# Attention and experts on one core: one written order for all engines per pair of heads

## The chip, the cores and the metric

The kernel runs on one core of a Trainium2 chip. The core has five engines that run side by side, each working through its own list of instructions in order: TensorE (PE in the profile, its weight loads PEld), VectorE (DVE), ScalarE (ACT), GpSimd (POOL) and SyncE (SP), which only issues DMAs. They wait for each other through semaphores. The metric is the time of one execution in microseconds (us), lower is better. TensorE's clock is granted at one of two levels, 1.2 or 2.4 GHz; the profile shows it as a share of full speed.

## The reference

Two stages follow each other. Attention has 8 batches of 8 heads, 576 tokens and head dimension 64; then a mixture of 8 experts picks one expert per token.

```python
    scores = scale * np.matmul(q, k.transpose(0, 1, 3, 2))
    log_f = np.log(np.clip(f, 0.0001, 1.0))
    cum = np.cumsum(log_f, axis=-1)
    decay = cum[:, :, :, None] - cum[:, :, None, :]
    scores = np.where(causal, -1000000000.0, scores + decay)
    scores = scores - np.max(scores, axis=-1, keepdims=True)
    attn = np.exp(scores)
    attn = attn / (np.sum(attn, axis=-1, keepdims=True) + 1e-09)
    return np.matmul(attn, v).astype(np.float32)
...
    logits = x @ w_gate
    expert_idx = np.argmax(logits, axis=1)
...
        h = np.maximum(xe @ w1[e], 0.0)
        ye = h @ w2[e]
        out[mask] = gate_w[mask, None] * ye
```

## The kernel before

Attention goes over 32 pairs of heads (`n` = 0 to 31, four pairs per batch), then the expert stage runs from about 450 us to the end. The change touches attention only, and the first steps of the expert stage that are mixed into its last pass.

The work of one pair has these pieces. The names in brackets are those of the new code, and this text uses them for both kernels.

- **Scores.** `s_tiles` (line 358) multiplies q with k for query tiles 3 (R1, 512 columns), 2 (R2, 384) and 1 with 0 (R3, 256 and 128), for both heads. `s_joint` (line 391) does the fifth, half-filled query tile of both heads together (J).
- **Row minima.** `reds` on DVE (line 342) reads each score bank, adds the decay bias, writes the result to SBUF tiles `sc` and leaves the row extreme in `nmx`. The names are r03 to r10 (head, tile), rj0 and rj1 for the joint tile.
- **Exponentials.** `exps` on ACT (line 377, joint tile 383): e03 to e10 and ej.
- **Turns.** The exponentials are transposed on PE in three groups of 16 half-turns (line 408): G1 (tile 3), G2 (tiles 2 and 1), G3 (the diagonal blocks and the joint tile). Each group fills two PSUM banks, which ACT or DVE copies to SBUF tile `aT` (line 420). One full turn of the joint tile (TL, line 403) is copied by DVE (tl, line 465).
- **Product with v.** `av` (line 475) writes two banks (AVa, AVb); ACT copies them to `xT` (line 483).

PSUM is handed out in a fixed rotation of seven banks (`next_bank`), so each piece that asks for banks waits until the bank taken seven requests earlier has been read.

The loop over `n` runs seven steps `s0` to `s6`. Per step it emits R1 with its minima (s0), G2 of the pair before (s1), R2 (s2), G3 of the pair before (s3), R3 (s4), TL and the product of the pair before, then J of this pair (s5), and G1 of this pair (s6). So on PE a pair reads: R1, G2, R2, G3, R3, TL, AV, J, G1. `order.pin()` after each step ties the instructions of each engine to the order in which steps were written; inside a step a scheduler chooses.

Behind the pieces of a pair come the tasks of the batch that was finished before (`fin_tasks`): the gate product (`fin_gate`, line 551), five tiles of normalised rows (`fin_x`, turns on PE and scaling on DVE at line 510), the gate's logits, softmax, expert choice, rank, slot, and the one-hot products `hi` (line 923 on DVE, then line 930 on POOL), `lo` (line 937) and `table` (line 944 on PE, added up on DVE at line 948). They are spread over four passes of the loop: of `n % 4`, 1 carries the gate, 2 two row tiles, logits, softmax and expert, 3 gate value, two row tiles, rank and slot, 0 the one-hots, the table and the last row tile. POOL also masks the bias of the next pair (lines 309 to 318) and splits q and k into two rounded parts (lines 293, 298).

## Time and profile before

| what | value |
|---|---|
| time, median of three runs | 890.74 us (889.8 to 891.26) |
| profiled execution, its own time | 893.72 us |
| its span, first to last instruction | 892.0 us |
| mean granted TensorE clock | 0.901 |
| PE busy | 838.8 us, 94% |
| DVE, ACT, POOL busy | 593.8, 478.4, 496.7 us |
| attention, first to last exponential of a joint tile | 17.7 to 428.3 us |

A row of the window view gives, for a stretch, its length and each engine's busy time; a busy engine may still be a slow one, since matmuls last longer at the lower clock. PEclk is the granted share of full clock in that stretch.

### The profile page before, as it was taken

The numbers are of one execution on the slowest core, as the hardware profiler recorded it, in microseconds if no ns is written. First come the engines' busy times: TensorE is split into PE (matmuls) and PEld (weight loads), VectorE is DVE, ScalarE is ACT, GpSimd is POOL, SyncE is SP. The second block draws the span as 40 slices with busy tenths as digits, with TensorE's granted clock in tenths as the row PEclk, the third lists the DMA queues.
The fourth block names the chain that finished last, engine by engine and source line by source line (L and its number), as shares of the span: only waits on it lengthen the run. The fifth ranks groups of instructions, "written<-read, shape, count | busy, mean of one in ns | idle before, by whom it ended". The sixth has DMA issues, their size and how long they took to land.

```text
span 892.0 us, 18923 instructions
## 1 busy us (share of the span) xinstructions
PE 838.8 (94%) x6640; PEld 683.5 (77%) x6640; DVE 593.8 (67%) x1707; ACT 478.4 (54%) x1216; POOL 496.7 (56%) x616
## 2 busy tenths in 40 slices
PE   5998999989989899898899999999999999999997
PEld 4676676666766666666788998988989899898985
DVE  6667676676776766767443887584966848588450
ACT  6775464655646546466353655554646546465430
POOL 6985472854628456366325676465755657566411
PEclk9998687877878778786799999999999999999999
DMA  7655353563644534445114453634335343443301
GB/s 189 168 150 150 109 160 102 133 163 96 161 116 134 159 100 146 146 137 174 58 64 147 124 164 98 198 96 141 84 111 178 95 159 86 128 128 107 115 12 41
DMA packets 78817, 112.15 MB, mean 126 GB/s; under 512 B 9343, under 2 KB 40063, under 8 KB 78720
## 3 DMA queue, kind: packets, MB, share of 16 engines
q1 hardware_dynamic: 71680, 90.97, 35.2%
q0 software_dynamic: 6400, 19.93, 6.9%
q8 instruction: 54, 0.88, 0.4%
q14 instruction: 43, 0.35, 0.1%
q10 hardware_dynamic: 640, 0.01, 0.0%
HBM read 91.85 MB, written 20.07 MB: 125 GB/s over the span
## 4 chain that ended last, share of the span: by engine, by line
PE 72%; DVE 13%; POOL 6%; issue 5%; DMA 2%; ACT 1%; ACTq 0%; DVEq 0%; SPq 0%; POOLq 0%
PE ps L1151 24%; PE ps L1349 16%; PE ps L475 13%; PE ps L358 5%; DVE sc L342 4%; PE ps L1121 4%; DVE aT L420 3%; PE ps L408 3%; PE ps L391 2%; PE ps L403 2%; DVE sc_J L342 2%; PE pr L1349 1%; POOL bias L309 1%; PE ps L1305 1%; POOL hl L298 1%
## 5 line engine op out<-in xcount | busy, mean ns | idle before, releaser
L377 ACT ACTIVATE sc<-sc,nmx 128x512 f32<-128x512 f32 (+3 forms) x256 | 143.4, 562 | 69.1 <-DVE nmx L342 67.2
L358 PE MATMUL ps<-hl 64*128 64x512 f32 (+3 forms) x768 | 124.4, 403 | 21.9 <-DVE nmx L342 14.0
L475 PE MATMUL ps<-aT,va_t 128*64 128x256 f32 (+3 forms) x896 | 128.2, 453 | 2.5 <-ACT sc L377 2.1
L1151 PE MATMUL ps<-w_0w,hhw 128*128 128x512 f32 x280 | 113.0, 404 | 0.0
L475 PEld LDWEIGHTS ps<-aT,va_t 128*64 128x64 f32 x896 | 74.8, 181 | 48.7 <-issue 27.9
L1349 PE MATMUL ps<-X_0w,w1s 128*128 128x320 f32 x504 | 111.7, 309 | 0.0
L1151 PE MATMUL ps<-w_0w,hl 128*128 128x512 f32 x280 | 110.9, 396 | 0.0
L1151 PE MATMUL ps<-w_1w,hhw 128*128 128x512 f32 x280 | 110.5, 395 | 0.0
L358 PEld LDWEIGHTS ps<-hl 64*128 64x128 f32 x768 | 80.9, 233 | 36.4 <-DVE nmx L342 14.2
L1159 POOL DMA_INDIRECT out<-y,si_fast x37 | 37.7, 1018 | 97.2 <-ACT y L1158 82.8
L420 DVE COPY aT<-ps 128x512 f32<-128x512 f32 (+1 forms) x160 | 87.7, 574 | 1.8 <-PE ps L408 1.6
L298 POOL TENSOR_TENSOR hl<-raw,hl 128x512 fp32r<-128x512 f32 (+1 forms) x62 | 83.3, 1344 | 5.1
L342 DVE CUSTOM_DVE_ANT_0 sc_J<-ps,bias 128x288 f32<-128x288 f32 x32 | 14.6, 458 | 105.4 <-PE ps L391 105.4
L1349 PEld LDWEIGHTS ps<-X_0w,w1s 128*128 128x128 f32 x504 | 84.3, 188 | 0.0
L1349 PE MATMUL ps<-X_1w,w1s 128*128 128x320 f32 x252 | 78.0, 310 | 0.0
L293 POOL CAST hl<-raw 128x512 fp32r<-128x512 f32 (+1 forms) x60 | 38.2, 637 | 62.1 <-DMA raw<-in_qkT 46.7
L1158 ACT ACTIVATE y<-ps,g_fast 128x512 f32<-128x512 f32 x37 | 25.5, 689 | 84.9 <-PE ps L1151 63.6
L483 ACT COPY xT<-ps 128x320 f32<-128x320 f32 x64 | 25.5, 399 | 80.6 <-PE ps L475 80.6
L930 POOL TENSOR_TENSOR Rr<-eqh,vals 128x240 bf16<-128x240 bf16 x35 | 19.4, 587 | 82.0 <-DVE eqh L923 82.0
L1151 PEld LDWEIGHTS ps<-w_0w,hl 128*128 128x128 f32 x280 | 52.5, 188 | 12.6
L1151 PEld LDWEIGHTS ps<-w_1w,hhw 128*128 128x128 f32 x280 | 52.9, 189 | 11.0
L1151 PEld LDWEIGHTS ps<-w_0w,hhw 128*128 128x128 f32 x280 | 52.6, 188 | 10.9
(240 smaller groups left out, 2033.3 us busy)
## 6 DMA issues: line engine op xcount, KB each, us to landing
bias<-ud SPq DMA_DIRECT2D x31, 576.0 KB, 5.6
w1r<-in_w SPq DMA_DIRECT2D x112, 128.0 KB, 3.4
w<-in_w SPq DMA_DIRECT2D x28, 512.0 KB, 5.0
raw<-in_qkT SPq DMA_DIRECT2D x64, 160.0 KB, 3.0
raw<-in_qkT SPq DMA_DIRECT2D x64, 144.0 KB, 3.0
va_t<-in_va SPq DMA_DIRECT2D x32, 256.0 KB, 5.7
x_dram<-row SPq DMA_DIRECT2D x32, 256.0 KB, 2.4
wraw<-in_w SPq DMA_DIRECT2D x7, 512.0 KB, 3.8
```

Of the source, the lines that this page charges most:

```text
L293: return eng(hls[n][:, 0, o : o + w], raws[n][:, r : r + w])
L298: return eng.tensor_tensor(hl[:, 1], raws[n][:, r : r + w], hl[:, 0].bitcast(F32), ALU.subtract)
L342: V.tensor_tensor_reduce(dst, src, in1, -0.125, init, ALU.add, ALU.min, nms[n][:, col : col + 1])
L358: note(nc.tensor.matmul(pb[j][:, o : o + w], hl[js, q, P * t : P * t + P], hl[js, k, 512 : 512 + w], start=(i == 0), stop=(i == 2),))
L377: A.activation(x, x, AF.Exp, bias=nms[n][:, 5 * j + t : 5 * j + t + 1], scale=-1.0, accum_out=ssums[b][:, t, 2 * p + j : 2 * p + j + 1])
L408: note(nc.tensor.transpose(out.bitcast(F32R), words, c.identr[rows, rows]))
L420: copy_on = {"a": lambda o, i: A.copy(o, i), "v": lambda o, i: V.tensor_copy(o, i)}
L475: note(nc.tensor.matmul(pv[j * HD : (j + 1) * HD, q0 - qa : qb - qa], l, r, start=(blk == 0), stop=(blk == nb - 1),))
L1121: c.note(nc.tensor.matmul(ph[:, 0:n], w[:, wi, fs], x[xi][:, kt, :], start=(k == 0), stop=(k == 3 * KT - 1),))
L1151: c.note(nc.tensor.matmul(py, rows(hi_, ft), w[wi], start=(ft + k == 0), stop=(ft == FT - 1 and k == 2),))
L1159: nc.gpsimd.indirect_dma_start(out=self.out, out_offset=bass.IndirectOffsetOnAxis(ap=si[:, s : s + 1], axis=0), in_=y, in_offset=None, bou ...
L1349: self.nc.tensor.matmul(bank[:, 0:HN], w[:, wi, mat, kt], x[xi][:, kt, :], start=start and k == 0, stop=k == 5, skip_group_check=True,)
```

## The change

The seven steps become one tuple `PERIOD` of about 55 entries, each a name, a lag in pairs (0 for this pair, 1 for the pair before) and a function. Every entry is emitted and pinned by itself, so the order inside a pair is now written out for all engines. Entries without a function (`at(...)`) are places where loads, masks, roundings and the tasks of the finished batch hang; a task carries the name of its place instead of a step number.

What the new order has that differs: G1 moves from the end of its own pair to the pass of the next pair, so that all three groups of turns are a pair late; on PE a pair reads R1, G1, R2, G2, G3, R3, J, TL, AVa, AVb. J now stands ahead of the product with v. Three exponentials (e01, e00, e10) are a pair late too. Of the bank copies, those of G1, G2 and all but one of G3 go to ACT and stand in one run ahead of this pair's exponentials; the two copies of the product with v go from ACT to DVE. The row tiles (`fx`) stand behind the product, softmax, expert and slot beside it (place V), logits, rank and table between R3 and J (place X), and the one-hots just ahead of the table in the same pass (place U). Row writes to DRAM wait six places instead of three steps, and five products of the first expert that were spread over the last pass stand at two places.

```diff
-            for half in range(2):
-                s_red(n, region(c.values, n, 0, -1)[:, half * JW : half * JW + JW],
-                      pb[half][:, 0:JW], added(n, half, -1), 10 + half,
-                      1.0e38 if half == 0 else nms[n][:, 10:11])
+                held[n, "j", half] = pb[half][:, 0:JW]
...
+        def av_last(n):
+
+            pvs[n] = [next_bank() for _ in range(2)][::-1]
+            lasts[n] = pvs[n][1][0:64, 256:384]
+            turn(lasts[n], region(c.words, n, 0, -1)[:, 512:S])
...
+        def av_out(n, part, eng):
             b, p = divmod(n, NPAIR)
...
+            qa, qb = ((0, 320), (320, S))[part]
+            copy_on[eng](xTs[b][:, p, qa:qb], pvs[n][part][:, 0 : qb - qa])
...
-                later.append([3, write])
+                later.append([6, write])
...
-                (0, 4, lambda: fin_gate(b)), (1, 4, lg[0]), (1, 4, lg[1]), (1, 5, softmax),
-                (1, 6, expert), (2, 0, gate), (2, 4, rank), (2, 5, slot), (2, 6, hi),
-                (3, 0, lo), (3, 4, table), (1, 1, fx[0]), (1, 3, fx[1]), (2, 1, fx[2]),
-                (2, 3, fx[3]), (3, 4, fx[4]),
+                (0, "X", lambda: fin_gate(b)), (0, "F", fx[0]), (0, "F", fx[1]),
+                (1, "X", lg[0]), (1, "X", lg[1]), (1, "V", softmax), (1, "V", expert),
+                (2, "U", gate), (2, "X", rank), (2, "V", slot), (3, "U", hi), (3, "U", lo),
+                (3, "X", table), (3 - 2 * late, "F", fx[2]), (3 - late, "F", fx[3]),
+                (3 - late, "C", fx[4]),
...
+        PERIOD = (
+            at(0), ("R1", 0, score(3)), ("e01", 1, power(0, 1)), ("e00", 1, power(0, 0)),
+            ("e10", 1, power(1, 0)), ("G1", 1, grouped(1, g_first)), at(1),
+            ("r03", 0, most(0, 3)), ("r13", 0, most(1, 3)), ("R2", 0, score(2)),
...
+        for n in range(NP + 1):
+            for name, lag, f in PERIOD:
+                if f is None:
...
+                    prepare(n, name)
+                    behind(n, name)
+                elif 0 <= n - lag < NP:
+                    step(lambda: f(n - lag))
                 order.pin()
...
-        return [lambda: moe.up(0, 0, i - 2)]
+        ups = {4: (0, 1, 2), 6: (3, 4)}.get(i, ()) if n == last + 1 else ()
+        return [lambda ft=ft: moe.up(0, 0, ft) for ft in ups]
```

The order that results is shown at three places. The first is PE in a pass with `n % 4` = 0, from the product with v on; `sc` are exponentials, `raw` unrounded q and k, `xT` the normalised rows' source, `hl` the rounded q and k. Before:

```order
L403 MATMUL ps<-identr,xT1w 64x128 x4
L403 MATMUL ps<-identr,sc_Jw 64x128
L475 MATMUL ps<-aT_97,va_t 64x320 x2
L475 MATMUL ps<-aT_97,va_t 64x192 x2
L475 MATMUL ps<-aT_97,va_t 64x64 x2
L475 MATMUL ps<-aT_97,va_t 64x256 x6
L475 MATMUL ps<-aT_97,va_t 64x192 x2
L475 MATMUL ps<-aT_97,vb_182 64x64 x2
L391 MATMUL ps<-raw 64x288 x4
L408 MATMUL ps<-identr,sc_03w 128x64 x8
L408 MATMUL ps<-identr,sc_13w 128x64 x8
L358 MATMUL ps<-hl 128x512 x6
```

The same place on PE in the changed kernel:

```order
L391 MATMUL ps<-raw 64x288 x4
L405 MATMUL ps<-identr,sc_Jw 64x128
L481 MATMUL ps<-aT_97,va_t 64x320 x2
L481 MATMUL ps<-aT_97,va_t 64x192 x2
L481 MATMUL ps<-aT_97,va_t 64x64 x2
L481 MATMUL ps<-aT_97,va_t 64x256 x6
L481 MATMUL ps<-aT_97,va_t 64x192 x2
L481 MATMUL ps<-aT_97,vb_182 64x64 x2
L405 MATMUL ps<-identr,xT1w 64x128 x4
L410 MATMUL ps<-identr,xT1w 128x64 x16
L358 MATMUL ps<-hl 128x512 x6
```

J moved from behind the product to ahead of it, the turns of G1 between J and R1 are gone from here (they stand behind R1 now), and three row tiles (`xT1w`) follow the product.

The second place is ACT in one plain pair, from its first exponential of tile 3 on. Before:

```order
L377 ACTIVATE sc_03_71,ssum<-sc_03_71,nmx 128x512
L420 COPY aT_91<-ps 128x2x2x2x64
L377 ACTIVATE sc_13_77,ssum<-sc_13_77,nmx 128x512
L420 COPY aT_91<-ps 128x4x64 x2
L377 ACTIVATE sc_02_73,ssum<-sc_02_73,nmx 128x384
L377 ACTIVATE sc_12_79,ssum<-sc_12_79,nmx 128x384
L377 ACTIVATE sc_01_75,ssum<-sc_01_75,nmx 128x256
L483 COPY xT_85<-ps 128x320
L377 ACTIVATE sc_11_81,ssum<-sc_11_81,nmx 128x256
L483 COPY xT_85<-ps 128x256
L377 ACTIVATE sc_02_73,ssum<-sc_02_73,nmx 128x128
L377 ACTIVATE sc_12_79,ssum<-sc_12_79,nmx 128x128
```

ACT in one plain pair of the changed kernel:

```order
L377 ACTIVATE sc_03_57,ssum<-sc_03_57,nmx 128x512
L377 ACTIVATE sc_11_67,ssum<-sc_11_67,nmx 128x256
L377 ACTIVATE sc_02_59,ssum<-sc_02_59,nmx 128x384
L377 ACTIVATE sc_13_63,ssum<-sc_13_63,nmx 128x512
L377 ACTIVATE sc_12_65,ssum<-sc_12_65,nmx 128x384
L383 ACTIVATE sc_J,jsum<-sc_J,nmx 128x576
L377 ACTIVATE sc_01_61,ssum<-sc_01_61,nmx 128x256
L377 ACTIVATE sc_02_59,ssum<-sc_02_59,nmx 128x128
L377 ACTIVATE sc_12_65,ssum<-sc_12_65,nmx 128x128
L422 COPY aT_91<-ps 128x2x4x64 x2
L422 COPY aT_91<-ps 128x2x2x2x64 x2
L422 COPY aT_91<-ps 128x4x64 x3
```

Five copies were strung between nine exponentials (three of `aT`, two of `xT`); now nine exponentials and seven copies of `aT` form two runs.

The third place is DVE in a pass with `n % 4` = 0, around the one-hots. Each minimum is followed by a small `nmx` row. Before:

```order
L420 COPY aT_97<-ps 128x2x4x64 x2
L923 TENSOR_TENSOR eqh<-pr,iotah 128x200
L650 MEMSET ssum 64x8
L342 ISA sc_03_57,nmx<-ps,bias 128x512
L342 ISA nmx 128x1
L342 ISA sc_13_63,nmx<-ps,bias 128x512
L342 ISA nmx 128x1
L937 TENSOR_TENSOR Ar<-pr,iota_601 128x640
L420 COPY aT_97<-ps 128x2x2x2x64
L420 COPY aT_97<-ps 128x4x64
L342 ISA sc_02_59,nmx<-ps,bias 128x384
L342 ISA nmx 128x1
```

DVE at the one-hots of the changed kernel:

```order
L342 ISA sc_12_65,nmx<-ps,bias 128x384
L342 ISA nmx 128x1
L913 TENSOR_TENSOR eqh<-pr,iotah 128x200
L927 TENSOR_TENSOR Ar<-pr,iota_606 128x640
L422 COPY aT_97<-ps 128x4x64
L938 TENSOR_TENSOR tab<-tab,pr 128x240
L342 ISA sc_02_59,nmx<-ps,bias 128x128
L342 ISA nmx 128x1
L342 ISA sc_01_61,nmx<-ps,bias 128x256
```

The one-hot `eqh` came ahead of the minima of tile 3 and the table's addition `tab` some twenty rows later; now `eqh` follows the minima of tile 2, and `tab` stands three rows behind it, ahead of the minima of tiles 0 and 1.

## Rows read from the trace of the kernel before

**Rows 1.** The page's slices: the span in 40 equal slices, busy share of PE and granted clock in tenths.

```profile
PE   5998999989989899898899999999999999999997
...
PEclk9998687877878778786799999999999999999999
```

**Rows 2.** The window view, one stretch per pair, from the joint tile's exponential of one pair to that of the next: length, then busy time (and count) of PE, PEld, DVE, ACT, POOL; granted clock, DMA share and GB/s. The first is an early pair without batch tasks, the others the four pairs of one batch (`n` = 17 to 20).

```profile
28.45:38.52 10.07, 9.05 (x117) 7.14 (x117) 7.11 (x27) 7.04 (x23) 9.54 (x18) 1.00 0.54 153
...
223.40:233.40 10.00, 9.78 (x131) 7.01 (x131) 7.01 (x27) 7.65 (x26) 6.44 (x10) 1.00 0.67 153
233.40:248.04 14.64, 13.84 (x146) 10.22 (x144) 10.49 (x41) 7.74 (x24) 8.52 (x13) 0.77 0.49 145
248.04:263.88 15.84, 13.73 (x131) 9.67 (x129) 11.15 (x49) 7.60 (x25) 3.91 (x4) 0.68 0.44 126
263.88:278.01 14.13, 12.86 (x124) 9.35 (x124) 9.80 (x38) 7.38 (x23) 11.15 (x19) 0.76 0.44 118
```

**Rows 3.** The view of line 383, the joint tile's exponential, one per pair: duration and first and last start.

```profile
L383 ACT ACTIVATE sc_J<-sc_J,nmx x32: 761/777/782, 17.7 to 428.3; 128x576 f32<-128x576 f32 x32
```

**Rows 4.** The window view again, the same batch cut at the turn TL (product with v and J follow it) and at the first turn of G1 (turns and scores follow it): columns as in rows 2.

```profile
222.50:228.46 5.96, 5.74 (x90) 4.44 (x88) 5.81 (x20) 4.32 (x14) 3.54 (x7) 1.00 0.54 142
228.46:232.48 4.02, 4.02 (x48) 2.55 (x41) 1.18 (x8) 3.31 (x13) 2.88 (x4) 1.00 0.86 170
232.48:240.73 8.25, 7.45 (x95) 6.38 (x94) 7.66 (x25) 5.38 (x16) 6.11 (x9) 0.80 0.55 142
240.73:246.39 5.66, 5.66 (x43) 3.27 (x42) 2.17 (x14) 2.23 (x9) 3.27 (x6) 0.69 0.41 155
246.39:256.92 10.53, 8.42 (x96) 6.78 (x95) 9.67 (x39) 5.36 (x16) 3.91 (x4) 0.72 0.63 170
256.92:263.01 6.09, 6.09 (x47) 3.50 (x45) 2.19 (x14) 2.38 (x9) 0.00 (x0) 0.64 0.11 43
263.01:271.20 8.19, 6.92 (x81) 5.85 (x80) 7.82 (x29) 4.90 (x14) 4.73 (x9) 0.81 0.62 161
271.20:277.09 5.89, 5.89 (x45) 3.46 (x43) 1.93 (x10) 2.47 (x11) 5.56 (x10) 0.68 0.21 59
```

**Rows 5.** The timeline of PE in the pair at 223 us: start, length, operation, count, idle time before it. A piece's length is read from one start to the next, since matmuls overlap.

```profile
223.16 0.97 PE L358 MATMUL ps<-hl 64*128 64x512 f32 x6
223.96 0.20 PE L408 MATMUL ps<-identr,sc_01w 64*128 64x64 f32 x2
...
224.55 0.80 PE L358 MATMUL ps<-hl 64*128 64x384 f32 x6
225.19 0.45 PE L408 MATMUL ps<-identr,sc_02w 64*128 64x64 f32 x4
...
226.52 0.91 PE L358 MATMUL ps<-hl 64*128 64x256 f32 x11 [0.22 <-DVE aT L420]
227.35 1.18 PE L551 MATMUL ps<-xT,wg 128*32 128x512 f32 x16
228.46 0.25 PE L403 MATMUL ps<-identr,sc_Jw 128*64 128x128 f32 x1
...
231.41 1.14 PE L391 MATMUL ps<-raw 128*64 128x288 f32 x8
```

**Rows 6.** Groups of ACT's copies in the pair from 48.42 to 58.52 us, shapes kept apart: count, busy us, mean ns, idle before.

```profile
L420 ACT COPY aT<-ps 128x256 f32<-128x256 f32 x2 | 0.6, 370 | 0.0
L420 ACT COPY aT<-ps 128x512 f32<-128x512 f32 x1 | 0.6, 566 | 0.0
L483 ACT COPY xT<-ps 128x320 f32<-128x320 f32 x1 | 0.4, 417 | 0.0
L483 ACT COPY xT<-ps 128x256 f32<-128x256 f32 x1 | 0.4, 372 | 1.2 <-PE ps L475 1.2
```

**Rows 7.** Groups of DVE's work in the same pair.

```profile
L420 DVE COPY aT<-ps 128x512 f32<-128x512 f32 x4 | 2.7, 688 | 0.0
L342 DVE CUSTOM_DVE_ANT_0 sc<-ps,bias 128x512 f32<-128x512 f32 x2 | 1.3, 688 | 0.0
L342 DVE CUSTOM_DVE_ANT_1 sc<-ps,bias 128x384 f32<-128x384 f32 x2 | 1.1, 548 | 0.0
...
L420 DVE COPY aT<-ps 128x256 f32<-128x256 f32 x2 | 0.8, 417 | 0.0
```

**Rows 8.** The one-hots and the table in the timelines of DVE, POOL and PE (start, length).

```profile
265.90 0.35 DVE L923 TENSOR_TENSOR eqh<-pr,iotah 128x200 bf16<-128x200 f32 x1
...
266.34 2.77 POOL L930 TENSOR_TENSOR Rr<-eqh,vals 128x240 bf16<-128x240 bf16 x5 [11.71 <-DVE eqh L923]
...
270.01 1.18 PE L944 MATMUL pr<-Rr,Ar 128*128 128x240 bf16 x5
```

**Rows 9.** The window view of three stretches of turns and scores: columns as in rows 2.

```profile
223.80:227.30 3.50, 3.28 (x54) 2.81 (x50) 3.50 (x11) 2.48 (x8) 1.30 (x4) 1.00 0.59 161
...
234.00:237.40 3.40, 2.90 (x51) 2.39 (x47) 3.29 (x9) 2.21 (x7) 1.56 (x4) 1.00 0.62 179
237.40:240.70 3.30, 3.00 (x28) 2.62 (x27) 2.96 (x11) 2.24 (x8) 3.14 (x4) 0.50 0.69 160
```

**Rows 10.** First and last instruction of softmax and expert choice in DVE's timeline (two copies of 1.28 us together lie between them).

```profile
247.19 0.20 DVE L848 TENSOR_REDUCE mx<-pr 128x5 f32<-128x40 f32 x1
...
249.96 0.21 DVE L870 CAST ohb<-pr 128x48 bf16<-128x48 f32 x1
```

More of the change, by code (lines that the diff above doesn't have):

```diff
@@ L395, in s_joint, with red_joint @@
                     ))
[L396 to L399 removed]
+                held[n, "j", half] = pb[half][:, 0:JW]
+        def red_joint(n, half):
+            s_red(n, region(c.values, n, 0, -1)[:, half * JW : half * JW + JW],
+                  held.pop((n, "j", half)), added(n, half, -1), 10 + half,
+                  1.0e38 if half == 0 else nms[n][:, 10:11])
         def turn(out, words):
@@ L481, in av_out, with out_last, av @@
-        def av_out():
-            A.copy(*pvs.pop(0))
+        pvs, lasts = {}, {}
+        def av_last(n):
+            pvs[n] = [next_bank() for _ in range(2)][::-1]
+            lasts[n] = pvs[n][1][0:64, 256:384]
+            turn(lasts[n], region(c.words, n, 0, -1)[:, 512:S])
+        def out_last(n):
+            V.tensor_copy(aTs[n][0:64, :, 1024:1088],
+                          lasts.pop(n).rearrange("p (j q) -> p j q", j=2))
+        def av(n, part):
+            va_t, vb_t = vts[n]
+            aT, pv = aTs[n], pvs[n][part]
+            qa, qb, nb = ((0, 320, 3), (320, S, 5))[part]
+            for blk in range(nb):
+                q0 = max(qa, P * blk)
+                for j in range(2):
+                    if blk < 4:
+                        l, r = va_t[:, blk, j, :], aT[:, j, AS * blk + q0 : AS * blk + qb]
+                    else:
+                        l, r = vb_t[:, j, :], aT[0:KB, j, 1024:1088]
+                    note(nc.tensor.matmul(
+                        pv[j * HD : (j + 1) * HD, q0 - qa : qb - qa], l, r,
+                        start=(blk == 0), stop=(blk == nb - 1),
+                    ))
@@ L638, in attention_all, with grouped, turned, score @@
         c.note = note
-        todo = None
-        for n in range(NP + 1):
+        todo, pts = None, {}
+        def grouped(k, f):
+            def turned(n):
+                pts[k, n] = f(n)
+            return turned
+        def score(*ts):
+            return lambda n: s_tiles(n, *ts)
+        def most(j, t):
+            return lambda n: reds(n, (j, t))
+        def power(j, t):
+            return lambda n: exps(n, (j, t))
+        def out(k, f, r, eng):
+            return lambda n: f(n, pts[k, n], r, eng)
@@ new lines, in prepare @@
+        def prepare(n, i):
+            if n + 2 < NP and i == 0:
+                load_raw(n + 2)
+            if n + 2 < NP and i == 2:
+                load_bias(n + 2)
+            if n == 0 and i == 0:
+                late_consts()
+                for part in (Q, K):
+                    rounded(1, A.copy, part)
+                for part in (Q, K):
+                    rest(1, G, part)
+            if n + 1 < NP and i == 1:
+                for f in selects(n + 1):
+                    f()
+            if n + 2 < NP and i in (3, 4):
+                part = (Q, K)[i - 3]
+                rounded(n + 2, G.tensor_copy, part)
+                rest(n + 2, G, part)
+            if i == 3 and 0 < n < NP:
+                load_v(n)
+            if i == 5 and n == 2:
+                load_gate()
+            if i in (2, 4) and 2 <= n < 5:
+                next(c.more, None)
@@ L641, in attention_all @@
             b, p = divmod(n, NPAIR)
-            new, old = n < NP, n > 0
-            m = n - 1
-            if new and p == 0:
+            if n < NP and (p, i) == (0, 0):
                 xTs[b], xTws[b] = (
@@ new lines, in behind @@
+        def behind(n, i):
+            nonlocal todo
+            b, p = divmod(n, NPAIR)
+            if n > 0 and (p, i) == (0, 0):
+                todo = fin_tasks(b - 1)
+            for f in tasks.pop((n, i), []):
+                step(f)
+            if n >= NPAIR:
+                if b == B:
+                    part = {1: 0, 3: 1, 5: 2}.get(i)
+                else:
+                    part = {(0, 1): 0, (1, 0): 1, (1, 4): 2}.get((p, i))
+                if part is not None:
+                    fin_sums(b - 1, part)
+            if (n, i) == (NP, 0):
+                scores.close()
+            if i in range(7):
```

153 lines of the change are left out of this document (23 added, 130 removed).

## The prediction

> **What bounds the kernel now.** I read the page's slices first: PE is busy in nine tenths of almost every slice, but its granted clock stands at 7 or 8 tenths from the fifth to the nineteenth slice, which is attention, and at full speed behind it [rows 1]. So the place to look is attention, and busy PE time there is partly slow PE time. The joint tile's exponential comes once per pair and runs from 17.7 to 428.3 us [rows 3]: 31 steps of 13.2 us on average. Cut by pairs, the window view shows what that mean hides. A pair with the clock at 1.00 takes 10.0 to 10.1 us, with batch tasks (223.40) or without (28.45); the other three of the same batch have a clock of 0.77, 0.68 and 0.76 and take 14.64, 15.84 and 14.13 [rows 2]. One batch is 54.6 us.
>
> Cut where the product with v begins and ends, each pair falls into a dense half (product and J: PE never idle) and a sparse half (turns and scores) [rows 4]. The dense half takes 4.02 us at full clock and 5.66, 6.09 and 5.89 in the other three pairs; the work is the same, so the clock costs 1.64 + 2.07 + 1.87 = 5.6 us per batch there. The sparse half takes 5.96, 8.25, 10.53 and 8.19 us, and in it DVE is busy for 5.81, 7.66, 9.67 and 7.82: 92 to 97%. In the dense half DVE is busy for only 1.2 to 2.2 us. So DVE bounds the sparse half, by minima, bank copies and batch tasks that all stand there, and then it sits idle while PE multiplies. PE's idle time in the sparse half is the other side of this.
>
> **What the clock does.** In the stretch 234.0 to 237.4 PE is busy for 2.90 of 3.40 us, with 51 matmuls that are mostly turns, and clock 1.00; in the next stretch it has 0.50 [rows 9]. At 223.8 PE is busy for 3.28 of 3.50 us with more score work, and the clock stays up in all of that pair. So what comes ahead of a fall is turns with waits between them, not idleness alone. The Trainium skill, "TensorE: Matmul & The Clock Gate", Part 4: PE-mode transpose, says that transposes do not count as PE activity in the way matmuls do; this trace agrees, with the 2.90 of 3.40 us just named. By the rule the new order, which sets G2 and G3 side by side, could lose the clock in every pair, which is worked out as the third rival (931 us); if PE's busy share alone decided, the clock would hold and the first rival's 806 us would follow.
>
> **The change part by part, for one batch.**
>
> PE's own work stays. From the starts in the pair at 223 us: R1 0.80, G2 0.59, R2 0.64, G3 0.73, R3 0.83, TL with the product 2.95, J 1.1 [rows 5], and G1, as many turns as G3, about 0.7. That is 8.3 us per pair at full clock. The batch tasks add the gate, 1.1 [rows 5]; four row tiles of 8 turns, half of G3 each, 1.5; the fifth, logits and rank, about 1.0 by their share of turns (estimate); the table, 0.6 (1.18 at half clock [rows 8]). So four pairs hold 33.2 + 4.2 = 37.4 us of PE.
>
> DVE loses three copies of 512 columns and one of 256, 3 x 0.688 + 0.417 = 2.48 us [rows 7], and gains two copies of the product, 320 and 256 columns. DVE has no copy of 320 in the trace; it lies between 0.417 and 0.688, I take 0.47. So 7.11 - 2.48 + 0.89 = 5.5 us in a plain pair. The batch tasks are what rows 2 show above 7.01: 3.48 + 4.14 + 2.79 = 10.4 us. Sum 4 x 5.5 + 10.4 = 32.5. What matters more is where: the minima of R3 and of J, both product copies, softmax, expert, slot and the row tiles now stand behind R3, in DVE's idle half.
>
> ACT gains three copies of 512 and one of 256 and loses two, 3 x 0.566 + 0.370 - 0.417 - 0.372 = 1.28 us [rows 6]: 7.04 + 1.28 = 8.3 us in a plain pair, 33.3 plus about 1 for gate and expert in a batch. POOL keeps its 6.44 + 8.52 + 3.91 + 11.15 = 30.0. So by work alone PE ends last, at 37.4, where 54.6 stand now.
>
> Then the waits that the fixed order adds; I followed one batch through the queues by hand, at full clock.
> - Pair with `n % 4` = 0: the one-hot on DVE now follows r12, so it ends about 3.8 us behind the start of R1 (R1 0.80, some 0.2 until DVE starts, two minima of 0.69 and two of 0.55, the one-hot 0.35 [rows 7, 8]). POOL needs 2.77 us more, until about 6.6. PE reaches the table at 0.80 + 0.70 + 0.64 + 0.59 + 0.73 + 0.83 = 4.3 and waits 2.3. Before, 3.8 us lay between the one-hot's end and the table [rows 8] and hid this. Behind the waiting table stand J and the product on PE, and behind `tab` on DVE the minima of R3, for which ACT's e11 waits too. Row tiles at the end hold a bank for another 0.4.
> - Softmax and expert, 250.17 - 247.19 - 1.28 = 1.7 us of DVE [rows 10], now stand ahead of rj1, so ej, then e01, e00, e10 and the copies of G1 are late by as much on ACT: G2, G3 and R3 of the next pair (`n % 4` = 3) wait about 1.2. Slot and gate value do the same to the pair after it, about 0.5, ahead of the table's wait.
> - A copy just ahead of AVa: 0.2.
>
> Waits 4.6 us, a batch of 42.0 at full clock. If the order hides all of them, 37.4; if each of the three pairs with routing waits as the table does (2.3, and 0.8 for what queues behind it), 37.4 + 9.3 = 46.7.
>
> Last the clock. The pair with the table has 2.3 us of waiting in turns and scores, so I expect it to lose the clock, and the one ahead of it (1.2 us of waits between G2 and G3) as well: two dense halves at 1.9 us more each [rows 4], 3.8, less a little that its ACT waits hide. The plain and the gate pair I expect at full clock: G1, R2, G2, G3 then follow each other without a wait between two score pieces. Bounds: 0 if it never falls, 5.6 if three dense halves stay as slow as today. I take 3.7: 42.0 + 3.7 = 45.7 us per batch.
>
> Pairs 6 to 31 are 6.5 batches: 6.5 x (54.6 - 45.7) = 58 us. The five early pairs run at full clock already; POOL is busy there for 9.54 of 10.07 us [rows 2], so I give them 3 us together. G1 of the last pair moves into the last pass (+0.7), which its five expert products, less scattered, may win back: 0. Row writes that wait longer, the other loads and GpSimd's masks keep their place ahead of need: 0, and at worst one wait of POOL for a bias, about 0.5.
>
> Sum against the profiled execution's 893.7: 893.7 - 58 - 3 = 832.7. That execution lies 3.0 above the median of the runs; at the median the forecast is 830 us. Between 43 and 48 us per batch it is 812 to 845.
>
> **Rivals.**
> 1. The clock holds throughout: 42.0 per batch, 893.7 - 6.5 x 12.6 - 3 - 3.0 = 806. For it: the pair at 223 us does hold its clock, with turns and a wait of 0.22 in it [rows 5], and DVE, which caused today's waits, is relieved. Against it: 2.3 us of waiting at the table.
> 2. The waits move rather than go: in-order queues pass DVE's routing chain on to ACT, which now does all copies ahead of its exponentials, and three pairs keep a slow dense half: 46.7 + 5.6 = 52.3, 893.7 - 6.5 x 2.3 - 6 = 873. For it: ACT at 8.3 us and PE at 8.3 in a plain pair leave no slack to either. Against: over a batch ACT has 8 us to spare below 42.0.
> 3. Slower: the clock falls in every pair, by turns standing side by side. Dense half 5.9 (mean of the slow three), sparse half with 2.3 us of score work doubled and 2.0 of turns kept, 6.6: 12.5 per pair, 50 per batch, plus tasks at half clock 4.2 x 1.5 and waits of 3, 59; early pairs 12.5 in place of 10.0. 893.7 + 6.5 x 4.4 + 5 x 2.4 - 3.0 = 931. Even at the lower clock part of this is hidden by waits. Time is lost from the point where a batch exceeds 54.6, three quarters of the way from 42.0 to 59. For it: [rows 9] and the page's rule on transposes. Against: R1 and R2 stand on both sides of G1, and the dense run of R3, J and product is one piece longer than today.
> 4. It does nothing, since another resource sets the end: POOL (30.0 of 54.6) and the DMA share of 0.44 to 0.67 [rows 2] do not look like it. 889 to 893.
>
> **How the numbers follow.** Forecast 50%, the first rival 18%, the second 15%, slower 13%, nothing 3%, better than all of these 1%. A difference below 0.2% (1.8 us, about the spread of the three runs) cannot be told from none. Faster holds forecast, first and second rival: 0.84; same 0.03; slower 0.13. The range reaches from below the first rival (40.0 per batch, 793) to just below the second (873): 792 to 872, which leaves out the slower side, nothing, and the tail below.
>
> **What would show it.** In the profile after, a batch of four pairs between 43 and 48 us; DVE's busy share of the sparse half well below 90%, and above half in the dense one; a wait of PE on POOL of about 2 us per batch at the table's line; waits of ACT for DVE in the pairs with softmax and gate value; two dense halves near 4.0 and two near 6 per batch. The forecast is wrong if the pairs without routing also show a clock below 1.00, if a batch stays above 50 us, or if PE waits for ACT's copies in every pair.

## The result, and the profile after

The changed kernel takes 809.41 us (median of 4 runs, 808.45 to 810.31), the kernel before 891.0 us on the same chip: a ratio of 0.9086, 95% interval 0.9071 to 0.9102. The forecast was 830 us, range 792 to 872. The profiled execution has a span of 807.3 us (892.0 before) and a mean granted clock of 0.979 (0.901 before).

The page's slices, PE busy and granted clock in tenths:

```profile
PE   5999999999999999969999999999999999999996
...
PEclk9999999989999999969999999999999999999999
```

Against [rows 1] the clock has no row of sevens and eights any more; the ninth slice stands at 8 and the eighteenth at 6. The eighteenth is the last pass of attention, which the joint tile's exponential shows to begin at 339.8 us instead of 428.3 [rows 3]:

```profile
L383 ACT ACTIVATE sc_J<-sc_J,nmx x32: 759/773/781, 17.9 to 339.8; 128x576 f32<-128x576 f32 x32
```

The window view, from one of these exponentials to the next: an early pair, then the four pairs of one batch (`n` = 17 to 20), then a stretch of the last pass (343.8 to 357.5). Columns as in [rows 2]: length, busy time (count) of PE, PEld, DVE, ACT, POOL, granted clock, DMA share, GB/s.

```profile
25.98:34.23 8.25, 8.25 (x117) 6.44 (x115) 5.83 (x24) 8.06 (x27) 7.87 (x15) 1.00 0.80 218
178.67:189.58 10.91, 10.48 (x151) 7.93 (x149) 7.94 (x30) 8.78 (x29) 8.32 (x13) 1.00 0.70 194
189.58:200.98 11.40, 10.82 (x150) 8.98 (x148) 9.64 (x44) 8.45 (x28) 7.35 (x10) 1.00 0.71 214
200.98:210.08 9.10, 8.95 (x119) 6.76 (x117) 8.36 (x43) 8.09 (x25) 6.12 (x8) 1.00 0.61 155
210.08:220.23 10.15, 9.24 (x114) 6.49 (x112) 7.14 (x28) 7.98 (x25) 8.46 (x14) 1.00 0.54 131
...
343.80:357.50 13.70, 7.47 (x42) 6.42 (x41) 1.27 (x3) 4.87 (x10) 7.99 (x10) 0.50 0.26 78
```

The batch takes 10.91 + 11.40 + 9.10 + 10.15 = 41.56 us, where [rows 2] add up to 54.6, and its clock is 1.00 throughout. PE is busy for 95% of it. Of the 26 pairs from `n` = 6 on, 22 have this clock; it falls in two table pairs (`n` = 12 and 28, 0.85), in one rank pair (`n` = 15, 0.69) and in a pair of the last batch (`n` = 30, 0.87). The early pair is 8.25 us of PE without a gap (10.07 with 9.05 busy before).

Cut as in [rows 4], now from R1 to J (turns and scores) and from J to the next R1 (J, product, row tiles), for the last three of these pairs:

```profile
190.72:195.39 4.67, 4.67 (x81) 4.35 (x79) 3.86 (x13) 3.86 (x14) 3.93 (x4) 1.00 0.80 235
195.39:200.21 4.82, 4.24 (x43) 2.97 (x42) 4.45 (x28) 3.35 (x12) 2.80 (x5) 1.00 0.64 199
200.21:205.46 5.25, 5.10 (x81) 4.32 (x79) 4.76 (x21) 4.57 (x17) 3.93 (x4) 1.00 0.68 155
205.46:209.63 4.17, 4.17 (x44) 2.66 (x42) 3.92 (x24) 3.26 (x11) 2.81 (x5) 1.00 0.45 137
209.63:216.41 6.78, 5.87 (x82) 4.49 (x78) 4.49 (x15) 5.94 (x19) 4.94 (x8) 1.00 0.70 171
216.41:220.58 4.17, 4.17 (x43) 2.67 (x42) 3.10 (x15) 2.75 (x9) 3.80 (x8) 1.00 0.34 91
```

The column of DVE, the third of the busy times, tells what moved. In the halves with turns and scores it is busy for 83, 91 and 66% (92 to 97% in [rows 4]); in the dense halves for 92, 94 and 74%, where it had 1.2 to 2.2 us to do. Its work was spread. PE's waits for DVE in the pairs from `n` = 6 on fall from 25.6 us in all to 4.0, and its idle time in the first kind of half is left almost in one place, the table (6.78 with 5.87 busy). PE, DVE, ACT and POOL there, from their timelines (start, length, operation, idle time before it):

```profile
214.26 0.56 PE L934 MATMUL pr<-Rr,Ar 128*128 128x240 bf16 x2
215.10 0.26 PE L934 MATMUL pr<-Rr,Ar 128*128 128x240 bf16 x1 [0.28 <-POOL Rr L920]
...
216.41 1.19 PE L391 MATMUL ps<-raw 128*64 128x288 f32 x8
```

```profile
212.93 0.36 DVE L913 TENSOR_TENSOR eqh<-pr,iotah 128x200 bf16<-128x200 f32 x1
...
216.50 0.41 DVE L938 TENSOR_TENSOR tab<-tab,pr 128x240 f32<-128x240 f32 x1 [1.62 <-PE pr L934]
```

```profile
213.37 2.77 POOL L920 TENSOR_TENSOR Rr<-eqh,vals 128x240 bf16<-128x240 bf16 x5 [0.89 <-DVE eqh L913]
```

```profile
217.83 0.51 ACT L377 ACTIVATE sc<-sc,nmx 128x256 f32<-128x256 f32 x1 [2.16 <-DVE nmx L342]
```

The table's five short matmuls (0.56 for two, 0.26 each) start at 214.26, the last three each wait 0.28 for their slice from POOL, and J starts at 216.41. DVE's addition stands behind them for 1.62 us, the minima behind that, and ACT's e11 behind those for 2.16: the chain that the prediction describes. PE's own idle time in it is 0.8 us.

Where the 84.7 us of span went, from the starts of the joint tile's exponentials: pairs 6 to 31 took 279.7 us instead of 359.7 (-80.0), the five early pairs 42.2 instead of 50.8 (-8.6); from the last of these exponentials to the end it is 467.5 us instead of 463.7 (+3.8), and the first comes 0.2 later.

### The profile page after: what moved, and what is told of

Its sections match the earlier page's. It is cut to its first block, busy times and chain, and to the rows that moved or that the text cites. A ratio compares the mean times of both kernels' runs of the same rounds, so it can differ in the third digit from the quotient of the medians.

```text
span 807.3 us, 18877 instructions
## 1 busy us (share of the span) xinstructions
PE 770.5 (95%) x6640; PEld 642.2 (80%) x6640; DVE 551.8 (68%) x1643; ACT 504.0 (62%) x1280; POOL 499.0 (62%) x616
## 4 chain that ended last, share of the span: by engine, by line
PE 77%; DMA 7%; POOL 6%; DVE 4%; issue 3%; ACT 2%; SPq 0%; POOLq 0%; DVEq 0%; ACTq 0%
PE ps L1141 27%; PE ps L1339 17%; PE ps L481 9%; PE ps L358 5%; PE ps L410 5%; PE ps L391 4%; PE ps L1111 3%; DMA bias<-ud 3%; DMA raw<-in_qkT 2%; POOL Rr L920 2%; PE ps L405 2%; PE pr L1339 1%; PE ps L1295 1%; PE ps L557 1%; POOL hl L298 1%
## 5 line engine op out<-in xcount | busy, mean ns | idle before, releaser
L377 ACT ACTIVATE sc<-sc,nmx 128x512 f32<-128x512 f32 (+3 forms) x256 | 141.7, 556 | 32.9 <-DVE nmx L342 32.6
L422 ACT COPY aT<-ps 128x512 f32<-128x512 f32 (+1 forms) x224 | 93.5, 505 | 15.8 <-PE ps L410 15.0
L481 PE MATMUL ps<-aT,va_t 128*64 128x256 f32 (+3 forms) x896 | 93.7, 361 | 4.2 <-PE ps L405 3.5
L358 PE MATMUL ps<-hl 64*128 64x512 f32 (+3 forms) x768 | 89.0, 347 | 3.9 <-DVE xT L422 2.5
L481 PEld LDWEIGHTS ps<-aT,va_t 128*64 128x64 f32 x896 | 59.5, 141 | 30.2 <-PE ps L405 4.1
L358 PEld LDWEIGHTS ps<-hl 64*128 64x128 f32 x768 | 59.1, 191 | 8.6 <-PE ps L410 3.0
L342 DVE CUSTOM_DVE_ANT_0 sc<-ps,bias 128x128 f32<-128x128 f32 (+1 forms) x128 | 59.3, 482 | 7.8 <-PE ps L358 3.0
L1141 PEld LDWEIGHTS ps<-w_0w,hl 128*128 128x128 f32 x280 | 52.5, 187 | 12.7
L1386 POOL TENSOR_TENSOR u<-u,u 128x320 f32<-128x320 f32 x27 | 23.7, 878 | 60.3 <-DVE u L1384 60.0
L309 POOL TENSOR_SCALAR_AFFINE_SELECT bias<-bias 64x576 f32<-64x576 f32 (+2 forms) x66 | 43.9, 665 | 25.8 <-ACT bias L260 6.8
```

Source lines behind the costliest of these rows:

```text
L309: G.affine_select(t[rows, BJ + c0 : BJ + c1], base[rows, j, c0:c1], [[-1, c1 - c0]], ALU.is_ge, NEG, base=512 - c0, channel_multiplier=1)
L342: V.tensor_tensor_reduce(dst, src, in1, -0.125, init, ALU.add, ALU.min, nms[n][:, col : col + 1])
L358: note(nc.tensor.matmul(pb[j][:, o : o + w], hl[js, q, P * t : P * t + P], hl[js, k, 512 : 512 + w], start=(i == 0), stop=(i == 2),))
L377: A.activation(x, x, AF.Exp, bias=nms[n][:, 5 * j + t : 5 * j + t + 1], scale=-1.0, accum_out=ssums[b][:, t, 2 * p + j : 2 * p + j + 1])
L422: copy_on = {"a": lambda o, i: A.copy(o, i), "v": lambda o, i: V.tensor_copy(o, i)}
L481: note(nc.tensor.matmul(pv[j * HD : (j + 1) * HD, q0 - qa : qb - qa], l, r, start=(blk == 0), stop=(blk == nb - 1),))
```

## The experiments

Each kernel was timed in rounds with the kernel before on the same chip; "after" is the changed kernel. The kernel before took 891.0 to 892.6 us in these rounds, so a difference of a microsecond or two between two experiments says nothing.

**1. The copies alone, in the old order.** From the kernel before; copies of G1, G2 and the joint tile go to ACT, the product's to DVE.

```diff
-            A.copy(*pvs.pop(0))
+            V.tensor_copy(*pvs.pop(0))
...
-                    out_second(m, second.pop(), 1, "v")
+                    out_second(m, second.pop(), 1, "a")
...
-                    out_joint(m, pt, 1, "v")
+                    out_joint(m, pt, 1, "a")
...
-                        out_first(n, pt, r, "v")
+                        out_first(n, pt, r, "a")
```

> The kernel before, in its old order, with the change's division of the bank copies alone: copies of G1, G2 and the joint blocks on ACT, the two copies of the product on DVE. Theory A (DVE's load in the sparse half is what cost the time): DVE loses 2.5 us a pair there, a batch falls from 54.6 to 46 to 49 us, 835 to 855 us in all, and the clock falls less often. Theory B (the order, above all J joined to the product and the tasks' places, is what gained): 880 to 895 us, or slower, since the copies now stand between ACT's exponentials.

844.27 us, ratio 0.9476 (0.9458 to 0.9495): theory A. The two pairs of a batch that carry rank and table, in the window view:

```profile
221.58:235.94 14.36, 12.75 (x137) 9.23 (x135) 10.51 (x51) 8.40 (x27) 3.90 (x4) 0.76 0.51 140
235.94:247.47 11.53, 10.94 (x127) 8.23 (x124) 8.07 (x29) 8.07 (x27) 10.64 (x19) 0.85 0.52 145
```

Relieving DVE alone brings 47 of the 82 us; the clock still falls (0.76 and 0.85) in the pairs with tasks.

**2. The new order with the old copies.**

```diff
-            ("g10", 1, out(1, out_first, 0, "a")), ("g11", 1, out(1, out_first, 1, "a")),
+            ("g10", 1, out(1, out_first, 0, "v")), ("g11", 1, out(1, out_first, 1, "v")),
...
-            at("V"), ("xa", 1, lambda n: av_out(n, 0, "v")),
+            at("V"), ("xa", 1, lambda n: av_out(n, 0, "a")),
```

(`g21`, `gj1` and `xb` likewise.)

> The changed kernel with the old division of the copies: G1 on DVE, one half of G2 and the joint blocks on DVE as before, the product's copies on ACT. Theory A: DVE is back at 7.0 us in a plain pair and bounds again, a batch of 46 to 50 us, 840 to 865. Theory B: the written order alone holds the gain, below 820.

869.43 us, ratio 0.9766 (0.9732 to 0.98). Theory A in kind, a little worse than its range: the order alone is worth 22 us, and taking the copies out of it costs 60, more than the 47 that they bring by themselves.

**3. The product's copies back on ACT, alone** (`xa` and `xb` of the diff above, nothing else).

> The two copies of the product with v go back from DVE to ACT, alone (about 0.8 us more per pair on ACT, 0.9 less on DVE). Theory A: ACT, at 8.0 to 8.8 us of a pair's 8.3 to 11.4, becomes the bound of the pairs without routing; 820 to 840 us, about a third to a half of the 60 us that all copies lost together. Theory B: they stand where ACT waits for DVE's minima anyway; 806 to 814 us, and the 60 us came from the copies of the turns alone.

815.41 us (808.3 to 816.83), ratio 0.9123 (0.9087 to 0.9159), which overlaps the changed kernel's interval. Theory A's 820 to 840 is out; whether it costs nothing or 6 us stays open, since its five runs fall into two at a mean clock of 0.98 (808 us) and three at 0.965 (815 to 817). The 60 us of experiment 2 came from the copies of the turns, or from both sets together.

**4. The tasks of the finished batch back near their old places.**

```diff
-                (0, "X", lambda: fin_gate(b)), (0, "F", fx[0]), (0, "F", fx[1]),
-                (1, "X", lg[0]), (1, "X", lg[1]), (1, "V", softmax), (1, "V", expert),
...
+                (0, "X", lambda: fin_gate(b)), (1, 2, fx[0]), (1, "T", fx[1]),
+                (1, "X", lg[0]), (1, "X", lg[1]), (1, 6, softmax), (1, 6, expert),
+                (2, 2, gate), (2, 2, fx[2]), (2, "T", fx[3]), (2, "X", rank), (2, 6, slot),
+                (2, 6, hi), (3, 2, lo), (3, "X", table), (3, "X", fx[4]),
...
-            ("g20", 1, out(2, out_second, 0, "a")), ("R3", 0, score(1, 0)), at(3),
+            ("g20", 1, out(2, out_second, 0, "a")), at("T"), ("R3", 0, score(1, 0)), at(3),
```

> The changed kernel with the batch tasks put back among the turns and scores: two row tiles behind G2 and G3 in two of the passes, softmax, expert, slot and one-hot ahead of the next pair's minima, one-hot therefore ahead of the table by most of a pair. Theory A: some 8 us of DVE work a batch return to the sparse half, PE waits there for DVE, the clock falls in two or three of four pairs, 840 to 865. Theory B: the clock is held by the dense run, so only the work moved counts, 805 to 820. If the table's wait is worth more than the row tiles' places it could even be faster than 809.

832.49 us, ratio 0.9349 (0.9329 to 0.937): between the two theories. Two effects of opposite sign are in it; the next run and experiment 9 measure one of them each.

**5. Four row tiles alone back among turns and scores.** Of the diff above only `fx[0]` to `fx[3]` and the place "T".

> Four of the five row tiles go back among turns and scores in the pairs that carried them before (two with logits, two with rank); softmax, expert, slot, one-hots and table stay where the change put them. Theory A: row tiles there take DVE time ahead of minima and put more turns side by side, and are most of the 23 us that all tasks lost together; 822 to 834 us. Theory B: the place of softmax, expert and slot was what mattered; 805 to 815 us.

852.27 us, ratio 0.954 (0.9521 to 0.956): theory A, at 43 us twice its size, and more than all tasks together lost. The four pairs of a batch, gate first:

```profile
197.11:206.76 9.65, 9.65 (x135) 7.06 (x133) 6.69 (x26) 8.79 (x29) 8.24 (x13) 1.00 0.70 168
206.76:219.74 12.98, 12.42 (x150) 9.67 (x148) 9.85 (x44) 8.50 (x29) 6.72 (x9) 0.87 0.60 182
219.74:233.00 13.26, 10.95 (x120) 7.50 (x117) 9.95 (x46) 8.19 (x25) 6.77 (x9) 0.74 0.54 150
233.00:246.45 13.45, 12.35 (x120) 7.82 (x118) 7.20 (x28) 8.31 (x25) 10.04 (x17) 0.75 0.42 113
```

and its waits between 60 and 330 us (us in total, times, the longest):

```profile
PE pr L876 <- DVE vals L869: 8.8, 6, 1.7
PE ps L410 <- DVE nmx L342: 6.5, 12, 0.6
```

The gate pair, freed of its two row tiles, is 1.3 us shorter; logits, rank and table pair are 1.6, 4.2 and 3.3 us longer at a clock of 0.87, 0.74 and 0.75. Ahead of the minima the row tiles make DVE late, and PE waits among turns for minima (`nmx`) and for the routing chain (`vals`). In experiment 4 the one-hot was early as well, and there the table pair held its clock (10.73 us at 1.00). By experiment 9 an early one-hot is worth about 15 us, and if the two effects simply add, which was not tested, 43 - 15 = 28 lies near the 23 measured in experiment 4.

**6. J behind the product again.**

```diff
-            ("J", 0, s_joint), ("r11", 0, most(1, 1)), at(4), ("TL", 1, av_last),
+            ("r11", 0, most(1, 1)), at(4), ("TL", 1, av_last),
...
-            ("rj0", 0, lambda n: red_joint(n, 0)), ("AVb", 1, lambda n: av(n, 1)), at(5),
+            ("AVb", 1, lambda n: av(n, 1)), ("J", 0, s_joint), at(5),
...
-            ("rj1", 0, lambda n: red_joint(n, 1)), ("e12", 0, power(1, 2)), at("C"),
-            ("xb", 1, lambda n: av_out(n, 1, "v")), at("F"), ("ej", 0, exp_joint), at(6),
+            ("e12", 0, power(1, 2)), at("C"),
+            ("xb", 1, lambda n: av_out(n, 1, "v")),
+            ("rj0", 0, lambda n: red_joint(n, 0)), ("rj1", 0, lambda n: red_joint(n, 1)), at("F"), ("ej", 0, exp_joint), at(6),
```

> The changed kernel with J behind the product instead of ahead of it, its minima behind the product's copies. Theory A: the sparse half and DVE's load in it stay, so 809 to 822 (the joint exponential is some 1.5 us later, which ACT may pass on to the turns). Theory B (the joined dense run holds the clock): the clock falls in most routing pairs, 830 to 850.

858.61 us, ratio 0.9637 (0.9619 to 0.9656): worse than either theory. The pairs with rank and table, and two waits:

```profile
223.66:234.76 11.10, 10.57 (x125) 7.78 (x121) 8.69 (x43) 8.09 (x25) 7.49 (x12) 0.85 0.57 137
234.76:252.62 17.86, 13.98 (x138) 9.34 (x136) 7.90 (x30) 8.08 (x25) 10.54 (x18) 0.71 0.41 99
```

```profile
ACT sc_J L383 <- DVE nmx L342: 45.1, 23, 4.8
...
DVE tab L939 <- PE pr L935: 17.8, 5, 4.5
```

J's minima come last, so ACT's ej waits for them (45.1 us in all; 7.6 in after), and what is behind ej on ACT, three exponentials and the copies of G1, is late for PE. In the table pair that joins the table's own wait: 17.86 us at 0.71, the longest of the six table pairs (15.5 at the least).

**7. G1 in its own pair again.**

```diff
-            ("e10", 1, power(1, 0)), ("G1", 1, grouped(1, g_first)), at(1),
+            ("e10", 1, power(1, 0)), at(1),
...
+            ("G1", 0, grouped(1, g_first)), at(6),
```

> G1 goes back to the end of its own pair, behind the joint tile's exponential in the written order; its two copies and everything else stay. Theory A: the exponentials of tile 3 are done by then, so the turns need not be a pair late; what the change gained lies in the copies, the place of J and the tasks, and the time stays within 800 to 818 us. Theory B: G1 in its own pair waits on PE for the exponential of the second head's tile 3, and the dense run ends in turns; a loss of 0.7 to 1.5 us per pair, 830 to 855 us.

840.99 us, ratio 0.941 (0.9387 to 0.9432): theory B's loss, though not by the wait that it named. The rank and table pairs:

```profile
220.42:230.07 9.65, 8.64 (x115) 6.46 (x113) 8.37 (x43) 8.19 (x26) 6.71 (x9) 1.00 0.55 146
230.07:242.11 12.04, 10.26 (x106) 6.56 (x106) 7.10 (x28) 8.18 (x26) 9.52 (x17) 0.86 0.43 115
```

PE waits little for exponentials of tile 3; it waits for a copy on ACT (8.4 us in nine waits between 60 and 330 us), and the table pair is 1.9 us longer at a clock of 0.86. This batch is the mildest: the other table pairs of the trace take 12.7 to 13.9 us, and in four of the seven rank pairs the clock falls as well (0.70 to 0.73).

**8. Copies strung between exponentials on ACT.** PE's and DVE's orders stay.

```diff
-            ("g10", 1, out(1, out_first, 0, "a")), ("g11", 1, out(1, out_first, 1, "a")),
+            ("g10", 1, out(1, out_first, 0, "a")), ("e03", 0, power(0, 3)),
+            ("g11", 1, out(1, out_first, 1, "a")),
...
+            ("e13", 0, power(1, 3)),
             ("g20", 1, out(2, out_second, 0, "a")), ("R3", 0, score(1, 0)), at(3),
             at("U"), ("g21", 1, out(2, out_second, 1, "a")),
+            ("e02", 0, power(0, 2)),
...
```

(The three exponentials leave their old places.)

> On ACT three exponentials (e03, e13, e02) move in between the bank copies, as the kernel before had them; PE's and DVE's written orders stay. Theory A: a bank that ACT copies 0.7 to 2 us later holds up PE's R3, J or the product in every pair, 825 to 850 us, with PE's wait for ACT's copies several times as large. Theory B: PE's seven banks give enough slack; within 4 us of the changed kernel, 805 to 813 us.

846.59 us, ratio 0.9484 (0.9466 to 0.9502): theory A. An early pair, and DVE's largest wait between 60 and 330 us:

```profile
45.40:54.80 9.40, 8.52 (x117) 6.67 (x115) 5.71 (x25) 8.18 (x25) 8.96 (x15) 1.00 0.56 158
```

```profile
DVE aT L422 <- ACT aT L422: 50.2, 23, 2.6
```

```profile
PE ps L391 <- DVE aT L422: 5.8, 12, 0.6
```

The early pair loses 1.15 us at full clock, 0.9 of it PE's idle time. The delay goes through DVE: the one bank copy that DVE kept waits for ACT's (14.0 us in after), with the minima of R3 queued behind it, and PE's J waits for the bank that this copy frees.

**9. The one-hot a pass earlier.**

```diff
-                (2, "U", gate), (2, "X", rank), (2, "V", slot), (3, "U", hi), (3, "U", lo),
+                (2, "U", gate), (2, "X", rank), (2, "V", slot), (2, "F", hi), (3, "U", lo),
```

> The one-hot hi moves one pass ahead (from the pass of the table to the one before it, behind the product), nothing else. Theory A: PE's wait of about 2.2 us at the table stands on the path in every batch, six or seven times; without it a batch of 41.6 becomes about 39.4, and the time falls by 13 to 16 us, to 793 to 798 us. Theory B (rival): what sets a batch's length is the sum of ACT's and PE's work, and the wait only fills time that would be waited elsewhere; the time falls by less than 4 us, 805 to 811 us, and PE's wait shows again at another line.

794.69 us, ratio 0.89 (0.8883 to 0.8917): theory A, so the table's wait did stand on the path. A table pair of experiment 11, which has the same edit:

```profile
122.40:131.10 8.70, 8.68 (x114) 6.52 (x112) 7.14 (x28) 8.02 (x26) 7.85 (x13) 1.00 0.62 158
```

It is 1.45 us shorter than after's 10.15, and PE has next to no gap left in it. Over the whole trace of experiment 11 the six table pairs inside attention take 52.9 us instead of 64.5 (two of after's had a fallen clock), and the stretch from the last joint exponential to the end 463.8 instead of 467.5, together 15.3; the span is 14.8 shorter. Experiment 9's own trace is of the slowest of its five executions (799.06 us; the others took 792.42 to 794.96). A rank and a table pair of it:

```profile
197.99:207.61 9.62, 9.45 (x107) 6.40 (x105) 8.46 (x42) 8.09 (x26) 3.45 (x4) 0.82 0.54 143
207.61:216.85 9.24, 9.24 (x126) 7.09 (x122) 7.31 (x28) 8.22 (x25) 7.53 (x13) 1.00 0.60 146
```

The table pairs are short here too (8.6 to 9.3 us), but the clock falls in six of the seven rank pairs (9.6 to 10.9 us; five of after's seven take 9.1 at 1.00), which gives part of the gain back in this execution. In experiment 11's trace it falls in three of them.

**10. Products of the first expert ahead of the last table.**

```diff
+            if i == "X":
+                for f in extra(n, i):
+                    step(f)
...
-        if (n, i) == (last + 1, 4):
+        if (n, i) == (last + 1, "X"):
...
-        ups = {4: (0, 1, 2), 6: (3, 4)}.get(i, ()) if n == last + 1 else ()
+        ups = {"X": (0, 1, 2), 6: (3, 4)}.get(i, ()) if n == last + 1 else ()
```

> Three products of the first expert move ahead of the last table, two places earlier in the last pass, so that PE has work while it waits for POOL's roundings of w2. Theory A: the last pass lost 3.8 us to PE's wait of 5.5 us there and the clock that fell with it; the time falls by 3 to 6 us, to 803 to 806 us. Theory B: the wait is set by the last rows themselves, and the products only change places: 807 to 811 us.

804.25 us (median of five executions between 800.73 and 805.68; a sixth took 820.32), ratio 0.9011 (0.8987 to 0.9036): theory A, about 5 us. In after PE's wait in the last pass reads

```profile
350.64 0.36 PE L934 MATMUL pr<-Rr,Ar 128*128 128x240 bf16 x1 [5.48 <-POOL Rr L920]
```

and the clock is 0.50 from 343.8, a little ahead of that wait, until 357.5. The one-hot was done at 343.5; POOL came to this product late because two steps that split the weights of the first expert (2.35 us each, the first waiting for ACT until 344.6) stand ahead of it.

**11. Edits 9 and 10 together.**

> Both edits together, hi a pass earlier and the products of the first expert ahead of the last table. If the two waits are separate places on the path, the gains add: 788 to 795 us. If the early hi already takes away the last pass's wait (or neither stands on the path), it equals the run with hi alone within 2 us.

794.24 us, ratio 0.8905 (0.8887 to 0.8923): the same as experiment 9. In experiment 9's trace PE's wait in the last pass is 1.1 us instead of 5.5, so the early one-hot had already taken most of it away. This is the best version found, about 15 us below after.

**12. Three groups of turns in a row.** R2 goes ahead of G1, so that 48 half-turns stand side by side.

```diff
-            ("e10", 1, power(1, 0)), ("G1", 1, grouped(1, g_first)), at(1),
-            ("r03", 0, most(0, 3)), ("r13", 0, most(1, 3)), ("R2", 0, score(2)),
+            ("e10", 1, power(1, 0)), ("R2", 0, score(2)), ("G1", 1, grouped(1, g_first)), at(1),
+            ("r03", 0, most(0, 3)), ("r13", 0, most(1, 3)), 
```

> R2 moves ahead of G1, so that PE reads R1, R2, G1, G2, G3, R3: 48 half-turns side by side instead of 16 and 32. Theory A: the clock falls only where PE also waits among turns; copies and minima keep pace, so the granted clock stays above 0.95 and the time lies within 805 to 825 us. Theory B (the third rival's mechanism): turns in a row without scores between them take the clock down in most pairs; mean granted clock below 0.93 and 840 us or more, up to 931.

818.46 us, ratio 0.9177 (0.9162 to 0.9192): theory A. An early pair and the rank pair:

```profile
44.90:53.40 8.50, 8.41 (x115) 6.57 (x113) 5.87 (x25) 8.11 (x27) 8.14 (x15) 1.00 0.67 179
...
207.43:216.53 9.10, 8.67 (x119) 6.75 (x117) 8.36 (x43) 8.09 (x26) 6.10 (x8) 1.00 0.61 156
```

Both hold the clock at 1.00 with all turns side by side, and so do all early and gate pairs from `n` = 2 on and six of the seven rank pairs. It falls in four of the six table pairs inside attention (two in after) and in two logits pairs, which have a wait of 0.2 us among the turns; another logits pair with the same wait keeps 1.00. So the order is 9 us slower than after without the third rival's fall in every pair.

## Why the prediction was right, and which terms were mis-sized

**The mechanism held.** The forecast was a gain of 61 us, and 82 came. That DVE in the half with turns and scores set the pace, and that copies on ACT, minima and tasks in the dense half free it, is what the windows show; experiment 1 takes work off DVE there and gains 47 us, experiments 2 and 5 give some back and lose 60 and 43. The work of the other engines per batch came as summed: DVE 33.1 us for 32.5, ACT 33.3 for about 34.3, POOL 30.3 for 30.0. The chain behind the table (`tab`, the minima of R3, e11) came as named; experiment 9 shows that it is on the path.

**The 42.0 us per batch met 41.56 by luck in part.** PE is busy for 39.5 us of it and idle for 2.1, where the sum had 37.4 of work and 4.6 of waits: two misses of over 2 us that cancel (busy time can hold short waits, since the ends of matmuls are modelled). The sum counted the table's wait, 2.3, and its five matmuls, 0.6, one behind the other; PE works on POOL's slices as they come, and from the first of the five to J it is 216.41 - 214.26 = 2.15 us for both. The late routing chain did make ACT wait, as named, but the 1.2 and 0.5 us that it was to cost PE in the next two pairs are not there: PE has no wait that the profile shows in the rank pair, and only POOL's in the table pair.

**Of the signs and readings,** DVE's share in the dense halves came (74 to 94% in the three pairs shown). In the other halves it is 66 to 91%, not well below 90% everywhere. The batch shown lies below 43 to 48 us, the mean of all at the lower edge, and no dense half of the batch shown is near 6 us. In [rows 1] the low clock reaches a slice further than the prediction read, to the twentieth, with a 6 in the fifth and the nineteenth; nothing rests on it.

**The clock term was too large.** I gave two slow dense halves to every batch, 3.7 us. In the trace shown the clock falls in four of the 26 pairs from 6 to 31, and all 26 take 279.7 us, 43.0 per batch, falls and the last batch's extra tasks included. Over 6.5 batches 45.7 - 43.0 is 17 us of the error. The first rival, in which the clock holds and to which I gave 18%, came nearest: 806 us. The range reached that far because it was drawn to take this rival in. The wait at the table that I held against it goes with a fallen clock in two of six table pairs; the rank pair of `n` = 15 falls without it, with no wait of PE above 0.3 us in it.

**The batch shown was a short one.** I took 54.6 us per batch for before; 359.7 us over 6.5 batches are 55.3. That is 5 us.

**The early pairs.** I gave them 3 us because POOL was busy for 9.54 of 10.07 us there; they gained 8.6. The step that failed took POOL's busy share for its work per pair. POOL's groups in the kernel before, from 28.45 to 68.5 us, which is four pairs:

```profile
L298 POOL TENSOR_TENSOR hl<-raw,hl 128x576 fp32r<-128x576 f32 x5 | 7.1, 1416 | 0.4
L309 POOL TENSOR_SCALAR_AFFINE_SELECT bias<-bias 64x576 f32<-64x576 f32 x10 | 6.7, 666 | 0.5
```

Five of a kind stand in four pairs (ten where a pair has two), and small constants of the expert stage beside them: POOL was running ahead of need. One pair's set is 2 x 0.67 + 1.42 + 1.28 + 0.67 + 0.61 + 0.64 + 0.51 + 0.41 = 6.9 us by the means of these groups, so POOL could not bound a pair of 8.25.

**The last pass** I put at nothing; it cost 3.8 us. I had G1's turns in that sum and not that PE waits at the table there too: it stands 5.5 us behind POOL. Either of experiments 9 and 10 is enough against it; in the trace of experiment 9 the stretch behind the last joint exponential is 461.8 us.

These four terms make up the miss: 17 + 5 + 5.6 - 3.8 = 24 us between the 832.7 of the sum and the 809.0 of the profiled execution.

**The rivals.** That the waits move to ACT (873) did not come: between 60 and 330 us PE waits for ACT's copies once, for 0.3 us. It goes that way when the copies are strung among the exponentials (experiment 8, through DVE) and when G1 is in its own pair (experiment 7). The slower rival (931) rested on turns side by side costing the clock, which the Trainium skill, "TensorE: Matmul & The Clock Gate", Part 4: PE-mode transpose, would lead one to expect; experiment 12 puts 48 half-turns in a row and keeps a clock of 1.00 in every early and gate pair from `n` = 2 on, so here turns in a row alone do not take it down. The prediction's sentence that the trace agrees with that page rested on one stretch (2.90 us busy of 3.40), which cannot tell the turns from the waits between them.

**The pieces do not add up, and the prediction's sum treated them as if they did.** Undone one at a time, the copies cost 60 us, J's place 49, the run of copies 37, G1's place 32 and the tasks 23: 201 us together, of a gain of 82. Each leaves PE waits that after has not or has shorter (for minima, for copies, for the table), and the clock falls in more of the pairs with tasks. The largest wait of PE left in after's attention is the table's, which experiment 9 removes.

## What to carry to other kernels

Where one engine is the bound in half of a loop and idle in the other, look for work that can change halves before looking for work to remove; the window view cut at the loop's own landmarks shows it. In a written order for in-order engines undo each piece alone before crediting it: here five pieces, given back one at a time, lost 28 to 73% of the whole gain each, and a sixth, the product's copies, at most 7%. A busy share is not the work per pass; count the instructions in the window first.
